# Filler products, split scores and values by DMA in the first chunk of a fused attention and feed-forward kernel

## The chip, the cores and the metric

The kernel runs on one core of a Trainium2 chip. The metric is device time in microseconds (us); lower is better. The core has five engines that work side by side, each through its own queue in order: TensorE (PE, matrix products, with its weight loads listed as PEld), VectorE (DVE), ScalarE (ACT), GpSimd (POOL) and SyncE (SP, which here issues every DMA). A float32 product is two instructions on PE in the profile, one in the type float32r is one.

## The reference

Windowed attention with block summaries, then a feed-forward layer with a squared ReLU. Batch 4, 8 heads, 768 positions, head size 64.

```python
k_sum = k.reshape(B, H, 24, 32, D).max(axis=3)      # block maxima of the keys
v_sum = v.reshape(B, H, 24, 32, D).mean(axis=3)     # block means of the values
scores_l = where(|i - j| < 16, q @ k.T / 8, -1e9)   # near keys
scores_s = q @ k_sum.T / 8 + log(32)                # block maxima
a = softmax(concatenate([scores_l, scores_s]))
x = (a @ concatenate([v, v_sum])) -> (3072, 512)
h = x @ w_in                                        # 512 -> 2048
out = (s * relu(h)**2 + b) @ w_out                  # 2048 -> 512
```

## The kernel before

The 3072 rows are cut into 12 chunks of 256 (`c`), three to a batch. A chunk's attention goes by head pairs `p` = 0..3: scores of four blocks of 64 queries against 96 near keys and 24 block maxima (`scores`), mask, scale and row minimum on DVE (`masked`), exponentials on ACT (`exps`), the division on DVE (`normalize`), transposes on PE (`transposes`), their copy on ACT (`turned`), products with 96 near values and 24 block means (`values`), and the copy of the result to the tile `x`, or to `xh` and `xl` (`attended`). The feed-forward layer walks 16 slices `f` of the hidden size: `hidden` (PE, tile `ph`), `activate` (ACT, then DVE in chunk 0, tiles `r` and `g`), `project` (PE, tile `po`), which runs two steps behind.

The weights arrive as 64-bit numbers in 32 tiles of 512 KB (`load_weights`, tile `wraw`). Each is scaled on ACT (`scale_weights`, two instructions, L116 and L117) and put together on DVE (`convert_weights`, L130, L132, L134, into `wf_in` or `wf_out`) while chunk 0 runs. Chunk 0 works in float32; later ones use two float32r halves.

The order of each engine's queue is written out by hand. `plan` maps a step to a list; within a step, entries are sorted by class (loads, splits, attention, weights, hidden, attention on PE, activation, projection, eviction), and nothing is reordered afterwards. Step -99 holds the string `FIRST_ORDER`, read from left to right: a letter is a stage, the digit its pair or weight slice.

- `q` loads keys and queries of a pair of chunk 0 (`kq`); `K` is `k_max` (L159), `S` both halves of `scores` (L269 near keys, L270 block maxima), `M` `masked` (L285), `E` `exps` (L298), `N` `normalize` (L305 to L308), `T` `transposes` (L314), `C` `turned` (L321).
- `r` loads rows of v (tile `vn`), `R0` to `R2` are products that average them (`mean_of_rows`, L202), `R3` copies the means to the tile `vsum` on ACT (L209).
- `v` loads near values into a tile `vw`, `F` is `fill_v` (L244: two copies that put each mean into `vw` four times, on DVE in chunks 0 and 1), `V` is `values` (L334), `X` `attended` (L347).
- `i`, `o` load weights; `A` scales one tile, `B` converts one, `D` two of a slice; `G0` is `fill_k` of chunk 1, pair 0 (L239); `u` loads queries and keys of a unit of chunk 1 (tile `qk`).

After that, step i runs `hidden`, `activate` for slice i of chunk 0, and chunk 1's attention is spread over steps 0 to 15 with offsets `lags`: its `scores(1,0)` stands on PE right behind `hidden(0,0)`, its four `fill_v` on DVE at steps 4, 7, 10 and 12, its loads of `vw` on SP at steps 0, 3, 6 and 8. The tile `vw` has four buffers, so the one of chunk 1, pair p comes free when `values(0,p)` is done. A tile pool with one buffer in PSUM (`ps_t`) holds the transposes.

Of the kernel before, what the change touches and what calls it, by code (L numbers as in the profile page):

```python
# [10 lines left out]
F32 = mybir.dt.float32  # L11
# [7 lines left out]
P = 128  # L19
B, H, S, D = 4, 8, 768, 64  # L20
# [3 lines left out]
SUB = 64  # L24
WIN = SUB + 2 * WINDOW
NB = S // BLOCK
KR = WIN + NB
NSUB = 4
# [11 lines left out]
def win_start(st):  # L40
    return min(max(SUB * st - WINDOW, 0), S - WIN)
# [3 lines left out]
def windowed_attention_then_relu2_ffn(ctx, tc, qk, vwin, kt, vt, kq, vrow, wp, sb, out):  # L45


    nc = tc.nc

    const = ctx.enter_context(tc.tile_pool(name="const", bufs=1))  # L50
# [8 lines left out]
    ps_t = ctx.enter_context(tc.tile_pool(name="ps_t", bufs=1, space=bass.MemoryType.PSUM))  # L59
# [6 lines left out]
    def make_mask(name, shifts):  # L66
        m = const.tile([P, KR], F32, name=name)
        nc.gpsimd.memset(m, 0.0)
        nc.gpsimd.memset(m[:, WIN:KR], 8.0 * math.log(BLOCK))
        for p0, shift in zip((0, 64), shifts):  # L70
            h = m[p0 : p0 + 64, 0:WIN]
            for sign in (1, -1):
                nc.gpsimd.affine_select(
                    out=h, in_=h, compare_op=ALU.is_gt, fill=NEG,
                    base=WINDOW + sign * shift, pattern=[[-sign, WIN]], channel_multiplier=sign,
                )
        return m

    mask_first = make_mask("mask_first", (0, WINDOW))
    mask_mid = make_mask("mask_mid", (WINDOW, WINDOW))  # L80
    make_identity(nc, ident)
# [7 lines left out]
    def at(step, order, fn, *args):  # L89
        plan[step].append((order, len(plan[step]), fn, args))  # L90
# [5 lines left out]
    for base, sign in ((0, 1), (BLOCK - 1, -1)):  # L96
        nc.gpsimd.affine_select(
            out=mean4[:, KR - 4 : KR], in_=mean4[:, KR - 4 : KR], compare_op=ALU.is_ge, fill=0.0,
            base=base, pattern=[[-sign * BLOCK, 4]], channel_multiplier=sign,
# [5 lines left out]
    def load_weights(key):  # L105
        side, f = key
        w_raw[key] = slots.tile([P, 512, 2], U32, name="wraw", tag="slot")
        src = wp[f, 0 if side == "in" else 1].bitcast(U32).rearrange("p (n w) -> p n w", w=2)
        nc.sync.dma_start(w_raw[key], src)
# [40 lines left out]
    kraw, ksum, vraw, vhalf, vsum = {}, {}, {}, {}, {}  # L150
# [42 lines left out]
    def load_scalars():  # L193
        nc.sync.dma_start(sb_col, sb.partition_broadcast(P))

    pm = []

    def mean_of_rows(n):
# [13 lines left out]
    def place(c):  # L212
        return c // PER_B, c % PER_B

    qk_t, vw_t, ps_of, pr_of, mn_of, sm_of, pt_of, pT_of, o_of, xt = ({} for _ in range(10))
# [7 lines left out]
    def load_unit(c, p):  # L223
        t = p3.tile([P, T + NSUB * KR], F32, name="qk", bufs=4)
        nc.sync.dma_start(t, qk[c - 1, p])
        qk_t[c, p] = t[:, 0:T], t[:, T:].rearrange("p (i k) -> p i k", k=KR)

    def load_values(c, p):
        v = p3.tile([KR, 2, NSUB, D], F32, name="vw", bufs=4)
        nc.sync.dma_start(v[0:WIN], vwin[c, p])  # L230
        vw_t[c, p] = v

    def filler(c):
        return nc.vector if c < 2 else nc.gpsimd
# [5 lines left out]

    def fill_v(c, p):
        bi, _ = place(c)
        for e in range(2):
            filler(c).tensor_copy(  # L244
                vw_t[c, p][WIN:KR, e],
                vsum[bi][WIN : WIN + NB, 2 * p + e, :].unsqueeze(1).to_broadcast([NB, NSUB, D]),
            )

    def scores(c, p, j):
        q, kw = qk_t[c, p]  # L250
        if j == 0:
            if c == 0 and p % 2:
                both = [ps_h.tile([P, T], F32, name="ps", tag="ph") for _ in range(2)]
                ps_of[c, p] = [t[:, : 2 * KR].rearrange("p (j k) -> p j k", k=KR) for t in both]
            elif c < 2:
                ps_of[c, p] = [ps_s.tile([P, 4, KR], F32, name="ps", tag="ps") for _ in range(2)]
            elif p % 2 == 0:
                both = [ps_s.tile([P, 4, KR], F32, name="ps", tag="ps") for _ in range(2)]
                ps_of[c, p], ps_of[c, p + 1] = [t[:, :2] for t in both], [t[:, 2:] for t in both]
        for e in range(2):  # L260
            r = slice(64 * e, 64 * e + 64)
            for a in range(2):
                i = 2 * j + a
                o, qi = ps_of[c, p][e][64 * a : 64 * a + 64, j], q[r, i * SUB : (i + 1) * SUB]
                if c > 0:
                    nc.tensor.matmul(o, qi, kw[r, i, :], start=True, stop=True)  # L266
                    continue
                w = win_start(i)
                nc.tensor.matmul(o[:, :WIN], qi, kraw[0, p][r, w : w + WIN], start=True, stop=True)  # L269
                nc.tensor.matmul(o[:, WIN:], qi, ksum[0, p][r], start=True, stop=True)  # L270

    def masked(c, p, j):
        _, ci = place(c)
# [129 lines left out]
    def evict(c):  # L403
# [8 lines left out]
    LOAD, SPLIT, ATT, WEIGHTS, HID, PE_ATT, CHAIN, PROJ, EVICT = range(9)  # L412


    FIRST, FIRST_SCALED, FIRST_TURNED = -100, 8, 2
    FIRST_ORDER = (
# [3 lines left out]
    )  # L420
    loads = {
        "q": load_first, "r": load_rows, "v": lambda p: load_values(0, p), "s": lambda _: load_scalars(),
        "i": lambda f: load_weights(("in", f)), "o": lambda f: load_weights(("out", f)),
        "u": lambda p: load_unit(1, p),
    }
    stages = {"K": k_max, "N": normalize, "F": fill_v, "T": transposes, "C": turned, "V": values, "X": attended}
    halves = {"S": scores, "M": masked, "E": exps}
    for n, name in enumerate(FIRST_ORDER.split()):
        kind, i = name[0], int(name[1:])
        if kind in loads:  # L430
            at(FIRST + 1, n, loads[kind], i)
        elif kind == "R":
            at(FIRST + 1, n, *((mean_of_rows, i) if i < 3 else (mean_done,)))
        elif kind == "A":
            at(FIRST + 1, n, scale_weights, ("in" if i % 2 == 0 else "out", i // 2))
        elif kind == "G":
            at(FIRST + 1, n, fill_k, 1, i)
        elif kind == "B":
            at(FIRST + 1, n, convert_weights, ("in" if i % 2 == 0 else "out", i // 2))
        elif kind == "D":  # L440
            at(FIRST + 1, n, convert_weights, ("in", i), ("out", i))
        elif kind in halves:
            for j in range(2):
                at(FIRST + 1, n, halves[kind], 0, i, j)
        else:
            at(FIRST + 1, n, stages[kind], 0, i)
    for c in range(1, NC):
        bi, ci = place(c)
        for p in range(NPAIR):
            if c == 1:  # L450

                base, v_at = (0, 3, 6, 8)[p], 0
                lags = (1, 2, 2, 3, 4, 4, 5, 6, 7)
            else:

                base, v_at = NF * (c - 1) - 2 + 8 * (p // 2), 3 * (p % 2)
                lags = ((1, 2, 2, 3, 6, 4, 5, 8, 9), (2, 3, 4, 5, 6, 6, 7, 8, 9))[p % 2]
            m, e0, e1, n, fv, tr, tu, va, xa = (base + lag for lag in lags)
            if ci == 0:
                at(base - 7, LOAD, load_k, bi, p)  # L460
                at(base - 2, ATT, k_max, bi, p)
                if p < 2:
                    for third in range(3):
                        at(base + v_at - 5 + third, LOAD, load_v, bi, p, third)
                        at(base + v_at - 1 + third // 2, ATT, v_sum, bi, p, third)
                    at(base + v_at + 1, ATT, v_mean, bi, p)
            if (c, p) not in ((1, 0),):
                at(base - 6, LOAD, load_unit, c, p)
            at(base + v_at, LOAD, load_values, c, p)
            if (c, p) != (1, 0):  # L470
                at(base - (1 if c > 1 else 2), ATT, fill_k, c, p)
            for j in range(2):
                at(base, PE_ATT, scores, c, p, j)
                at(m, ATT, masked, c, p, j)
                at((e0, e1)[j], ATT, exps, c, p, j)
            at(n, ATT, normalize, c, p)
            at(fv, ATT, fill_v, c, p)
            at(tr, PE_ATT, transposes, c, p)
            at(tu, ATT, turned, c, p)
            at(va, PE_ATT, values, c, p)  # L480
            if c < 2 or p % 2 == 0:
                at(xa, ATT, attended, c, p)
# [10 lines left out]
    for i in range(NC * NF):  # L493
        c, f = divmod(i, NF)
# [64 lines left out]
```

## Time and profile before

| what | value |
|---|---|
| median of 3 runs | 651.89 us (650.99 to 652.12) |
| the profiled execution | 652.11 us, span 650.4 us |
| busy share of the span | PE 97%, weight loads 85%, DVE 51%, ACT 51%, POOL 23% |
| DMA | 63.25 MB, mean 97 GB/s over the span |
| granted TensorE clock, mean | 0.997 |

The page divides the span into 40 slices of 16 us. PE shows 6 and 7 tenths in the first two and 9 or more in the others; DMA moves 324 to 389 GB/s in the first four slices and far less afterwards; DVE and ACT are full in slices three to five. So the first 90 us differ from the rest: there the weights arrive and are converted.

### The profile page before, as it was taken

What the parts mean: (1) busy time and instruction counts of PE and PEld (TensorE: products, weight loads), DVE (VectorE), ACT (ScalarE), POOL (GpSimd) and SP (SyncE); (2) the same over time, 40 slices, a digit from 0 to 9 for tenths busy, and PEclk for the clock granted to TensorE, in tenths of its full rate; (3) what the DMA queues carried; (4) which work ended last, traced back from release to release, by engine and by line L of the source; (5) the groups of instructions that cost most, each with busy time, mean ns of one, the idle gap of its engine ahead of it and who ended that gap; (6) DMA issues with size and microseconds to landing.
All of it is one profiled execution on the core that took longest, in us unless ns stands there. A gap on an engine that the chain in (4) does not pass through costs nothing.

```text
span 650.4 us, 13951 instructions
## 1 busy us (share of the span) xinstructions
PE 633.2 (97%) x5164; PEld 551.1 (85%) x5164; DVE 333.8 (51%) x1102; ACT 331.1 (51%) x972; POOL 152.5 (23%) x324
## 2 busy tenths in 40 slices
PE   6799999999999999999999999999999999999997
PEld 3565568899999999999999999999998989999996
DVE  5799997876433434356434344356443343342221
ACT  3899958745436435445445345254444444443322
POOL 3000004233133132231331331331322312312221
PEclk9999999999999999999999999999999999999999
DMA  8999405035203203224402300403510320100000
GB/s 324 389 386 349 122 2 185 2 102 184 78 1 104 72 3 126 59 76 142 146 1 65 112 1 33 154 10 119 179 56 2 105 71 2 57 3 1 32 2 33
DMA packets 25604, 63.25 MB, mean 97 GB/s; under 512 B 3968, under 2 KB 3968, under 8 KB 25536
## 3 DMA queue, kind: packets, MB, share of 16 engines
q1 hardware_dynamic: 25536, 62.36, 29.0%
q8 instruction: 41, 0.67, 0.4%
q14 instruction: 27, 0.22, 0.1%
HBM read 55.90 MB, written 6.29 MB: 96 GB/s over the span
## 4 chain that ended last, share of the span: by engine, by line
PE 88%; DVE 9%; DMA 1%; issue 1%; ACT 1%; SPq 0%; DVEq 0%
PE po L398 39%; PE ph L364 38%; PE pav L334 4%; PE ps L266 3%; PE pt L314 3%; DVE wf_in L132 1%; DVE wf_out L134 1%; DVE wf_out L132 1%; PE pm L202 1%; DMA vn<-in_vrow_dram 1%; DVE wf_in L134 1%; DVE wf_in L130 1%; DVE wf_out L130 1%; DVE g L375 1%; DVE vw L244 1%
## 5 line engine op out<-in xcount | busy, mean ns | idle before, releaser
L371 ACT ACTIVATE r<-ph 128x256 f32<-128x256 f32 x192 | 73.5, 383 | 286.4 <-PE ph L364 248.1
L381 DVE CAST gh<-g 128x256 fp32r<-128x256 f32 x176 | 52.7, 299 | 288.9 <-POOL g L379 262.1
L379 POOL TENSOR_SCALAR g<-r,sb_col 128x256 f32<-128x256 f32 x176 | 100.4, 570 | 423.8 <-ACT r L372 354.4
L398 PE MATMUL po<-wh,gl 128*128 128x512 f32 x352 | 142.9, 406 | 0.0
L398 PE MATMUL po<-wh,gh 128*128 128x512 f32 x352 | 138.7, 394 | 0.0
L398 PE MATMUL po<-wl_out,gh 128*128 128x512 f32 x352 | 138.1, 392 | 0.0
L364 PEld LDWEIGHTS ph<-xh,wl_in 128*128 128x128 f32 x704 | 107.6, 188 | 16.0 <-ACT r L372 0.7
L364 PE MATMUL ph<-xh,wl_in 128*128 128x256 f32 x704 | 113.1, 283 | 0.0
L364 PE MATMUL ph<-xl,wh 128*128 128x256 f32 x704 | 109.2, 277 | 0.0
L364 PE MATMUL ph<-xh,wh 128*128 128x256 f32 x704 | 108.8, 277 | 0.0
L364 PEld LDWEIGHTS ph<-xl,wh 128*128 128x128 f32 x704 | 95.1, 189 | 0.0
L364 PEld LDWEIGHTS ph<-xh,wh 128*128 128x128 f32 x704 | 92.9, 188 | 0.0
L372 ACT ACTIVATE r<-r 128x256 f32<-128x256 f32 x192 | 80.2, 418 | 6.1
L383 DVE TENSOR_TENSOR gl<-g,gh 128x256 fp32r<-128x256 f32 x176 | 76.4, 434 | 6.0
L398 PEld LDWEIGHTS po<-wh,gh 128*128 128x128 f32 x352 | 66.2, 188 | 13.8
L398 PEld LDWEIGHTS po<-wh,gl 128*128 128x128 f32 x352 | 66.1, 188 | 11.0 <-DVE gh L381 2.9
L398 PEld LDWEIGHTS po<-wl_out,gh 128*128 128x128 f32 x352 | 66.3, 188 | 7.8
L298 ACT ACTIVATE pr<-pr,mn 128x120 f32<-128x120 f32 x176 | 67.1, 383 | 3.4 <-DVE mn L285 3.4
L364 PEld LDWEIGHTS ph<-x,wf_in 128*128 128x128 f32 x128 | 24.8, 199 | 15.9 <-issue 6.3
L244 POOL COPY vw<-vsum 24x256 f32<-24x256 f32 x80 | 36.6, 497 | 1.3
L364 PE MATMUL ph<-x,wf_in 128*128 128x256 f32 x128 | 32.4, 400 | 4.5 <-DVE wf_in L134 3.7
L298 ACT ACTIVATION_READ_ACCUMULATOR pr<-pr,mn 128x1 f32 x176 | 33.1, 188 | 0.0
(70 smaller groups left out, 606.2 us busy)
## 6 DMA issues: line engine op xcount, KB each, us to landing
wraw<-in_wp_dram SPq DMA_DIRECT2D x32, 512.0 KB, 10.0
qk<-in_qk_dram SPq DMA_DIRECT2D x44, 368.0 KB, 5.1
vw<-in_vwin_dram SPq DMA_DIRECT2D x48, 192.0 KB, 4.9
out_dram<-o SPq DMA_DIRECT2D x24, 256.0 KB, 2.0
kraw<-in_kt_dram SPq DMA_DIRECT2D x12, 384.0 KB, 3.1
vraw<-in_vt_dram SPq DMA_DIRECT2D x12, 252.0 KB, 4.1
kq<-in_kq_dram SPq DMA_DIRECT2D x4, 512.0 KB, 4.3
vraw<-in_vt_dram SPq DMA_DIRECT2D x6, 264.0 KB, 6.8
```

Of the source, the lines that this page charges most:

```text
L244: filler(c).tensor_copy(vw_t[c, p][WIN:KR, e], vsum[bi][WIN : WIN + NB, 2 * p + e, :].unsqueeze(1).to_broadcast([NB, NSUB, D]),)
L266: nc.tensor.matmul(o, qi, kw[r, i, :], start=True, stop=True)
L298: nc.scalar.activation(pr, pr, AF.Exp, bias=mn_of[c, p][:, n : n + 1], scale=-1.0, accum_out=sm_of[c, p][:, n : n + 1])
L314: nc.tensor.transpose(pt_of[c, p][:KR, n * P : (n + 1) * P], pr[:, n, :], ident)
L334: nc.tensor.matmul(o[64 * e : 64 * e + 64, i * SUB : (i + 1) * SUB], vw[:, e, i, :], pT[:, e * T + i * SUB : e * T + (i + 1) * SUB], start ...
L364: nc.tensor.matmul(ph, w[:, kc * P : (kc + 1) * P], x[:, kc], start=(n == 0), stop=(n == len(terms) - 1))
L371: nc.scalar.activation(r, ph, AF.Relu)
L372: nc.scalar.activation(r, r, AF.Square)
L379: nc.gpsimd.tensor_scalar(g, r, s_col, b_col, ALU.mult, ALU.add)
L381: nc.vector.tensor_copy(gh, g)
L383: nc.vector.tensor_tensor(gl, g, gh.bitcast(F32), ALU.subtract)
L398: nc.tensor.matmul(po[t], a[:, t * P : (t + 1) * P], w, start=(f == 0 and n == 0), stop=(f == NF - 1 and n == len(terms) - 1),)
```

## The change

Five things change in chunk 0's start and in chunk 1:

1. DVE writes a tile of ones. New entries `W` (`keep_warm`) issue products of that tile with itself into the PSUM buffer of the transposes; nothing reads them. `W8` stands ahead of the first scores, `W1` behind those of pair 0, `W3` behind those of pair 1.
2. The products with the block maxima leave `scores` and become entries of their own, `Z`, so that near-key products no longer stand behind `k_max`.
3. The order of `FIRST_ORDER` changes: `R0` moves behind the scores of pair 2, `R1` behind the first transposes, `B0` ahead of the fills, `G0` behind `D1`, `u1` ahead of `i4`.
4. Chunk 1's four `load_values` move from steps 0 to 8 to entries `y0` to `y3` around `i5 o5`.
5. Chunk 1's `fill_v` becomes two DMAs on SP for each pair (24 rows, four times 256 bytes each), in place of two copies on DVE.

```diff
+    ones = const.tile([P, P], F32, name="ones")
+    nc.vector.memset(ones, 1.0)
...
+    def keep_warm(n):
+
+        t = ps_t.tile([P, 4 * P], F32, name="warm", tag="pt")
+        for _ in range(n):
+            nc.tensor.matmul(t[:, :P], ones, ones, start=True, stop=True)
+
...
     def fill_v(c, p):
         bi, _ = place(c)
+        if c == 1:
+            means = vsum[bi][WIN : WIN + NB, 2 * p : 2 * p + 2, :].unsqueeze(2).to_broadcast([NB, 2, NSUB, D])
+            for e in range(2):
+                nc.sync.dma_start(vw_t[c, p][WIN:KR, e], means[:, e])
+            return
...
+    def scores_of_maxima(p):
+        q, _ = qk_t[0, p]
+        for i in range(NSUB):
+            for e in range(2):
+                r = slice(64 * e, 64 * e + 64)
+                o = ps_of[0, p][e][64 * (i % 2) : 64 * (i % 2) + 64, i // 2]
+                nc.tensor.matmul(o[:, WIN:], q[r, i * SUB : (i + 1) * SUB], ksum[0, p][r], start=True, stop=True)
...
                 nc.tensor.matmul(o[:, :WIN], qi, kraw[0, p][r, w : w + WIN], start=True, stop=True)
-                nc.tensor.matmul(o[:, WIN:], qi, ksum[0, p][r], start=True, stop=True)
...
-        "K0 S0 K1 S1 M0 E0 K2 i2 M1 E1 o2 R0 S2 N0 T0 C0 K3 M2 E2 S3 i3 u0 N1 T1 R1 C1 M3 E3 R2 N2 T2 A0 C2 o3 i4 o4 "
-        "N3 T3 R3 C3 F0 V0 F1 X0 V1 F2 B0 A1 X1 V2 F3 X2 V3 B1 X3 A2 A3 G0 D1 i5 o5 A4 A5 A6 A7"
+        "W8 K0 S0 W1 Z0 K1 S1 Z1 M0 E0 W3 K2 i2 M1 E1 o2 S2 Z2 R0 N0 M2 E2 K3 S3 Z3 u0 i3 T0 R1 C0 N1 M3 E3 R2 A0 N2 T1 C1 o3 u1 i4 o4 "
+        "B0 T2 R3 C2 N3 F0 V0 F1 T3 X0 V1 F2 C3 X1 V2 F3 A1 X2 V3 B1 X3 A2 A3 D1 G0 y0 y1 i5 o5 y2 y3 A4 A5 A6 A7"
...
+        "u": lambda p: load_unit(1, p), "y": lambda p: (load_values(1, p), fill_v(1, p)),
...
-            if (c, p) not in ((1, 0),):
+            if (c, p) not in ((1, 0), (1, 1)):
                 at(base - 6, LOAD, load_unit, c, p)
-            at(base + v_at, LOAD, load_values, c, p)
+            if c != 1:
+                at(base + v_at, LOAD, load_values, c, p)
...
-            at(fv, ATT, fill_v, c, p)
+            if c != 1:
+                at(fv, ATT, fill_v, c, p)
```

More of the change, by code (lines that the diff above doesn't have):

```diff
@@ L423, in windowed_attention_then_relu2_ffn @@
         "i": lambda f: load_weights(("in", f)), "o": lambda f: load_weights(("out", f)),
-        "u": lambda p: load_unit(1, p),
+        "u": lambda p: load_unit(1, p), "y": lambda p: (load_values(1, p), fill_v(1, p)),
     }
@@ L435, in windowed_attention_then_relu2_ffn @@
             at(FIRST + 1, n, scale_weights, ("in" if i % 2 == 0 else "out", i // 2))
+        elif kind == "W":
+            at(FIRST + 1, n, keep_warm, i)
+        elif kind == "Z":
+            at(FIRST + 1, n, scores_of_maxima, i)
         elif kind == "G":
```

## The prediction, made before the changed kernel ran

> **What bounds the kernel now.** I read the page first, then a table of stretches of time, then PE's waits, then the engines' rows for the first 50 us. From the page:
>
> ```profile
> PE 633.2 (97%) x5164; PEld 551.1 (85%) x5164; DVE 333.8 (51%) x1102; ACT 331.1 (51%) x972; POOL 152.5 (23%) x324
> ```
>
> PE bounds the whole: what it waits, and what it does slowly, is the only time to win. The table shows where (length, then PE, PEld, DVE, ACT, POOL busy, granted clock, DMA share, GB/s):
>
> ```profile
> 8.00:25.95 17.95, 14.18 (x157) 8.49 (x157) 11.95 (x51) 11.44 (x40) 0.00 (x0) 1.00 1.03 373
> 25.95:50.00 24.05, 21.46 (x102) 14.20 (x100) 23.38 (x65) 23.79 (x58) 0.00 (x0) 0.93 1.03 391
> 50.00:76.00 26.00, 24.91 (x144) 15.88 (x144) 25.77 (x71) 23.67 (x60) 1.15 (x2) 1.00 0.88 275
> ```
>
> Up to 25.95 no engine is full: it is a chain of handovers. From 25.95 to 50 DVE, ACT and DMA are full together (23.38 and 23.79 of 24.05, share 1.03), and PE waits a little for each. So an earlier start counts only as far as all of them follow. PE's waits (total, times, longest):
>
> ```profile
> PE ph L364 <- DVE wf_in L134: 3.7, 4, 1.9
> PE pav L334 <- DVE vw L244: 1.5, 2, 1.2
> ...
> PE ph L364 <- ACT r L371: 0.7, 1, 0.7
> ```
>
> All of them fall before 88 us, so what PE has won by then stays won to the end. PE's own rows:
>
> ```profile
> 25.95 1.99 PE L364 MATMUL ph<-x,wf_in 128*128 128x256 f32 x8
> 27.87 0.64 PE L266 MATMUL ps<-qk 64*64 64x120 f32 x16
> 30.45 5.41 PE L364 MATMUL ph<-x,wf_in 128*128 128x256 f32 x16 [1.94 <-DVE wf_in L134]
> ...
> 50.73 0.45 PE L364 MATMUL ph<-x,wf_in 128*128 128x256 f32 x1 [1.00 <-DVE wf_in L134]
> ```
>
> `hidden(0,0)` starts at 25.95; the next waits 1.94 for its weights, and 16 instructions then take 5.41 where 8 took 1.99. The clock of that stretch, from the table:
>
> ```profile
> 31.00:32.00 1.00, 1.00 (x4) 0.82 (x3) 1.00 (x3) 1.00 (x3) 0.00 (x0) 0.50 1.05 405
> ```
>
> **The start, step by step.** PE is slow once more before that:
>
> ```profile
> 8.82 3.74 PE L202 MATMUL pm<-vn,mean 128*120 128x512 f32 x4 [0.92 <-DMA vn<-in_vrow_dram]
> ...
> 16.24 3.60 PE L202 MATMUL pm<-vn,mean 128*120 128x512 f32 x8
> 19.68 0.60 PE L314 MATMUL pt<-ident,pr 128*120 128x128 f32 x4
> ```
>
> `R0` takes 0.93 an instruction, `R1` and `R2` 0.45. So the clock is at half speed at 8.82 and full at 16.24 (the table's clock column reads 1.00 at 8.82, so it does not show this). Unbroken work opens it, and a pause of 2 us can shut it.
>
> `W8` is eight float32 products, 16 instructions. Four transposes of 128x128 take 0.45 to 0.60 at full speed, 0.11 each where they follow each other, so 0.23 at half speed and 3.7 in all. Bounds: 1.8 (full speed) and 7.4 (weight load not overlapped); I take 3.7, since the transposes have a load and a product of that size. With the ones written near 0.8, W8 runs from 1.1 to 4.7. The keys of pair 0 land at 4.3 and PE waits for them anyway: W8 costs 0.4 on the path, 3 us at the upper bound. `S0 W1 Z0 S1 Z1 W3` keep PE without a pause to 8; the clock opens between 4.5 and 8. From there the chain goes by rows such as these, of DVE and of ACT:
>
> ```profile
> 10.21 0.95 DVE L159 TENSOR_REDUCE ksum<-kq 128x24 f32<-128x768 f32 x1
> 13.75 0.28 DVE L285 CUSTOM_DVE_ANT_0 pr<-ps,mask_first 128x120 f32<-128x120 f32 x1 [2.59 <-PE ps L270]
> ```
>
> ```profile
> 16.93 0.40 ACT L298 ACTIVATE pr<-pr 128x120 f32<-128x120 f32 x1
> ...
> 18.45 0.66 ACT L116 ACTIVATE wraw<-wraw 128x512 f32<-128x512 f32 x1
> 19.01 0.67 ACT L117 ACTIVATE wraw<-wraw 128x512 int32<-128x512 uint32 x1
> 20.31 0.59 ACT L321 COPY pT<-pt 120x512 f32<-120x512 f32 x1 [0.63 <-PE pt L314]
> 20.92 0.58 ACT L209 COPY vsum<-pm 24x512 f32<-24x512 f32 x1
> ```
>
> `K` 0.95, `M` 0.9 (four of about 0.2), `N` 1.0, `E` 1.6, `A` 1.13, `C` and `R3` 0.59, `R1` with `R2` 3.43, `T` 0.45, `V` 0.65, `X` 0.3, `B` 1.9:
> - DVE: K1 to 6.5, M0 7.5, K2 8.4, M1 9.2, N0 10.2, M2 11.0, K3 12.0; Z3 on PE to 12.35. R0 lies beside this (8.7 to 10.6) and no longer holds pair 2's scores to 12.56.
> - PE: T0 12.8, R1 and R2 to 16.25, T1 16.7. ACT: E3 15.0, A0 16.15, C1 17.3, R3 17.9, C2 18.5.
> - DVE: B0 15.65 to 17.5, N3 18.45, fills (0.5 a pair) to 20.45. PE: V0 18.95 to 19.6, T3, V1, V2, V3 to 22.0. ACT: A1 to 22.1, X2 and X3 22.7.
>
> So `hidden(0,0)` starts at 21.9 for 25.95, **4.05 earlier**, and ACT is free of X3 at 22.7 for 26.4, 3.7 earlier. DVE before:
>
> ```profile
> 27.22 0.20 DVE L239 COPY qk<-ksum 128x96 f32<-128x96 f32 x1
> 27.34 0.42 DVE L130 TENSOR_SCALAR wf_in<-wraw 128x512 uint32<-128x512 uint32 x1
> 28.16 0.43 DVE L130 TENSOR_SCALAR wf_out<-wraw 128x512 uint32<-128x512 uint32 x1 [0.41 <-ACT wraw L116]
> ```
>
> D1's second tile waits for ACT's A3 at 28.16 and DVE is full from there on. A3 is now half done at 24.45: DVE is also **3.7 earlier**.
>
> **What speaks against it: G0.** The row at 27.22 is `G0`, which `scores(1,0)` needs. It now stands behind D1, which ends at 24.45 + 2.75 = 27.2. PE is done with `hidden(0,0)` at 23.7 and waits 3.7, to 27.4, where it waited 1.94, and all of PE's queue stands behind those scores. The weights of `hidden(0,1)` are there at 26.75; it starts at 28.3. The clock shuts in such a pause. With half speed to about 32 (eight at 0.45, eight at 0.235) the second and third hidden products end at 33.8 for 35.86: PE keeps **2.05**. Bounds: 2.55 if the clock opens at 30.8, 0.95 if at 34.2.
>
> The Trainium skill, "TensorE: Matmul & The Clock Gate", Part 1 (The HAM clock gate), says that the clock halves after an idle window of about 3.4 us, and that the windows run freely. Here it shut after a pause of 1.94, so the trace is stricter than the page. By the page a pause of 3.7 rarely covers a whole window, the clock would mostly stay open, and the sum would be that of the open-clock rival below.
>
> **Fills and loads by DMA.** The copies, as a group and in the chain that ended last:
>
> ```profile
> L244 DVE COPY vw<-vsum x16: 282/283/291, 21.5 to 82.3; 24x256 f32<-24x256 f32 x16
> ```
>
> ```profile
> 46.20 0.33 DVE g L375
> 46.53 0.03 issue
> 46.56 0.50 DVE vw L244 x2
> ```
>
> Eight of the 16 are chunk 1's. Two cost 0.50 and handovers of 0.03 on a full DVE, so each pair leaves 0.55: 2.2 in all, at steps 4, 7, 10, 12.
>
> The price is on DMA. SP has eight transfers out at a time, so an issue tells when the eighth before it landed:
>
> ```profile
> 26.31 6.31 SPq L109 DMA_DIRECT2D wraw<-in_wp_dram  x6
> 33.53 0.33 SPq L230 DMA_DIRECT2D vw<-in_vwin_dram  x1
> 34.48 0.33 SPq L225 DMA_DIRECT2D qk<-in_qk_dram  x1
> 35.82 0.33 SPq L109 DMA_DIRECT2D wraw<-in_wp_dram  x1
> ```
>
> ```profile
> 41.37 0.68 ACT L116 ACTIVATE wraw<-wraw 128x512 f32<-128x512 f32 x1
> ```
>
> `i6` was issued at 26.31, landed near 35.82 and was scaled at 41.37: 5.5 in hand. Now ACT comes 3.7 earlier, and four `vw` (0.79 MB at about 0.405 MB/us: 1.95) and eight fills stand ahead of it. A fill is 96 pieces of 256 bytes. The nearest rows are the copies of 24 such pieces, by their issue and by the DMA share while they run alone:
>
> ```profile
> L183 SPq DMA_DIRECT2D vsum<-vmean x24: 713/718/1221, 148.5 to 459.9; - x24
> ```
>
> ```profile
> 151.50:152.00 0.50, 0.50 (x5) 0.46 (x4) 0.50 (x1) 0.23 (x1) 0.47 (x1) 1.00 0.06 12
> ```
>
> 12 GB/s for 0.5 us is one copy of 6 KB, in 6% of 16 engines: 20 ns a piece. 768 pieces are 1.0 over 16 engines. Upper bound: SP's 0.72 for each fill as if nothing ran beside it, 5.8. I take 1.0, since seven other transfers are out while SP issues. Then `i6` lands at 38.8, 1.1 after ACT would take it at 37.7. `u1` ahead of `i4` (0.37 MB, 0.9) uses up the reserve of `o3` to `o4` and costs ACT some 0.4. SP itself: `y0` stands behind V0 (19.6) and `y3` behind V3 (22.0), both before SP has room for them (from about 24), so those waits are hidden; if V3 came after 32, SP would starve the weights queued behind it.
>
> ACT's lead thus falls to 2.4 around `i6`. Its `r` feeds `g` on DVE, and `g` of slices 0 to 2 comes hard behind its `r`: I take 0.4 off DVE's lead for it, an allowance. DVE is then 3.3 ahead, and with the fills gone 3.85, 4.4 and more.
>
> **Sum for PE.** 2.05 in front. Of the waits of 3.7 on DVE, 1.94 is spent again at G0; 1.74 go, and the 0.69 on ACT: 2.05 + 1.74 + 0.69 = 4.48, capped by DVE's 4.4. Less 0.2 for handovers: 4.2. The profiled execution was 652.11 (span 650.4), 0.22 above the median of 651.89: 652.11 - 4.2 = 647.9, by the median 647.7; I say **647.8**.
>
> **Rivals.** *The products do not open the clock early.* For it: the table does not show this gate at the start, and products that fill little of PE may not count. Against: the work from 8.82 on opened it before. R0 would take 3.74 from 10.0, Z3 ends 1.9 later, and PE keeps 0.15 + 1.74 + 0.69: 649.5.
>
> *Fills half hidden.* At 0.3 to 0.6 each, `i6` lands 1.4 to 3.8 later still and DVE waits on `g`: 649 to 651.5.
>
> *The fills starve ACT (slower).* `g` of slice 3 ran at 46.20; behind `i6` stand two tiles (2.4) and `r` (0.8), so `g` is later than before if `i6` lands after 43.0, that is, if a fill holds the stream for over 0.65. For it: SP's 0.72. Against: 6% busy. At 0.72 to 0.9 it lands at 43.5 to 45, and the kernel takes 652.4 to 653.5. The Trainium skill, "DMA: Bandwidth & Descriptors", Specifications, asks for 512 bytes a piece for line rate, which speaks for this rival; the row's 20 ns do not.
>
> *The clock stays open and DMA is no later.* PE then follows DVE's 5.0 to 5.7: 646.4 to 647.1.
>
> *The lead is lost on the way,* to a wait that I do not see: within 0.2% of before.
>
> **Numbers.** Mine 0.58 (646.9 to 648.9, by the clock's bounds and DVE's cap); clock late 0.08; half hidden 0.14; slower 0.07; open clock 0.10; lost 0.03. The range that leaves out under 2 in 10 is 646.4 to 650.3. A difference under 0.2% (1.3 us) cannot be told from none. Faster: 0.58 + 0.08 + 0.10 + 0.12 of the half hidden = 0.88; same 0.05; slower 0.07.
>
> **What would show it.** R0 at 0.45 an instruction, near 9; `hidden(0,0)` near 22; `scores(1,0)` waiting some 3.7 for L239, and half clock behind it; no L244 on DVE after 21; `i6` landing near 39; no PE wait on L134 after 35. I am wrong if V3 or the tiles of slices 4 to 7 come later than said, or if W8 lasts beyond 6.

## The result and the profile after

| | before | after |
|---|---|---|
| median | 652.00 us (6 runs, 650.99 to 652.40) | 655.56 us (6 runs, 654.10 to 657.61) |
| ratio, 95% interval | | 1.0056 (1.0043 to 1.0069) |
| profiled execution (span) | 652.11 us (650.4) | 657.61 us (655.9) |

The kernel is 3.6 us slower; the forecast was 4.2 faster, with 650.3 as the upper end. The profiled execution of after was the longest of its six, 2.05 above the median, so its pauses are a little longer than the median's. Three executions on record (one of before, one each of `e_undo45` and `e_pool_vw128`, 704 to 1611 us) ran far slower than all others and count in no ratio.

The page, engine by engine. PE's busy time is 5.3 us more than before, and its 24 further instructions are the fillers, of which `W8` takes 3.78:

```profile
PE 638.5 (97%) x5188; PEld 557.0 (85%) x5188; DVE 331.8 (51%) x1095; ACT 332.4 (51%) x972; POOL 153.2 (23%) x324
```

PE's waits from 20 to 100 us (total, times, longest). Before had 3.7 on the converted weights in four pieces; now there is one of 6.1:

```profile
PE ph L384 <- DVE wf_in L136: 6.1, 1, 6.1
PE ps L287 <- DVE qk L247: 3.2, 1, 3.2
PE ph L384 <- ACT r L391: 0.9, 1, 0.9
```

(In the changed kernel L384 is `hidden`, L247 `fill_k`, L118 and L119 `scale_weights`, L132 to L136 `convert_weights`, L391 to L395 `activate`, L111 `load_weights`, L238 `load_values`, L233 `load_unit`, L254 the fills' DMAs.) PE's rows in order of time, in brackets the pause ahead of the row and who ended it:

```profile
1.12 3.78 PE L202 MATMUL warm<-ones 128*128 128x128 f32 x16 [1.12 <-DVE ones L80]
9.39 1.98 PE L210 MATMUL pm<-vn,mean 128*120 128x512 f32 x4
13.35 3.60 PE L210 MATMUL pm<-vn,mean 128*120 128x512 f32 x8
18.06 0.65 PE L334 MATMUL pt<-ident,pr 128*120 128x128 f32 x4 [0.68 <-ACT pT L341]
19.59 0.88 PE L354 MATMUL pav<-pT,vw 120*64 120x64 f32 x16 [0.88 <-DVE vw L257]
21.32 2.81 PE L354 MATMUL pav<-pT,vw 120*64 120x64 f32 x48
24.07 1.99 PE L384 MATMUL ph<-x,wf_in 128*128 128x256 f32 x8
29.29 0.64 PE L287 MATMUL ps<-qk 64*64 64x120 f32 x16 [3.23 <-DVE qk L247]
29.86 5.41 PE L384 MATMUL ph<-x,wf_in 128*128 128x256 f32 x16
46.41 1.99 PE L384 MATMUL ph<-x,wf_in 128*128 128x256 f32 x8 [0.93 <-ACT r L391]
56.23 3.75 PE L384 MATMUL ph<-x,wf_in 128*128 128x256 f32 x8 [6.10 <-DVE wf_in L136]
```

The fillers do open the clock: `R0` takes 1.98 where it took 3.74. `hidden(0,0)` starts at 24.07 (before 25.95), but of that lead only 0.59 is left at `hidden(0,1)` (29.86 for 30.45). Then slice 6 starts at 56.23, where before had it at 50.73: 5.5 behind. It also takes 3.75 where an earlier eight took 1.99, because the clock shut in the pause (granted clock 0.50 from 55 to 60). That is 7.3 us behind. Before's later pauses of 0.36, 0.69 and 0.45 are gone, 1.5 of the 1.8 by which this exceeds the growth of the span, 5.5.

Who holds PE for 6.10 is in the chain that ended last, here from 42.96 on:

```profile
42.96 10.41 DMA qk<-in_qk_dram
53.37 0.02 issue
53.39 0.21 DVE qk L247
53.60 0.34 DVE wf_in L132
```

It is not a weight tile. It is `qk`, the queries and keys of chunk 1's third pair (`u2`, 0.37 MB), 10.41 us from issue to landing. On DVE, which works in order, the copy `fill_k` (53.39) stands ahead of the conversion of slice 6. It waits 5.33 for `qk`, and slice 6's weights wait behind it:

```profile
DVE qk L247 <- DMA qk<-in_qk_dram: 5.3, 1, 5.3
DVE g L395 <- ACT r L392: 2.6, 4, 1.1
```

Why `u2` lands so late stands in SP's queue (start, time on SP):

```profile
24.44 0.33 SPq L111 DMA_DIRECT2D wraw<-in_wp_dram  x1
25.70 0.33 SPq L238 DMA_DIRECT2D vw<-in_vwin_dram  x1
26.96 1.83 SPq L254 DMA_DIRECT2D vw<-vsum  x2
...
38.29 1.63 SPq L254 DMA_DIRECT2D vw<-vsum  x2
39.97 2.93 SPq L111 DMA_DIRECT2D wraw<-in_wp_dram  x6
42.96 0.43 SPq L233 DMA_DIRECT2D qk<-in_qk_dram  x1
```

From 25.70 to 39.97 SP works through `y0` to `y3` with `i5 o5` between. `i6` (39.97) had been issued at 26.31 before. `u2` had been issued at 34.48, a row that the prediction shows and does not use; now it goes out at 42.96, behind six tiles of 512 KB. The table by stretches (length, PE, PEld, DVE, ACT, POOL busy, granted clock, DMA share, GB/s) shows that the stream of loads itself became slower in that time; before it moved 406 and 407 GB/s in the first two of these stretches:

```profile
30.00:35.00 5.00, 5.00 (x16) 4.11 (x17) 4.92 (x18) 3.59 (x7) 0.00 (x0) 0.66 0.80 217
35.00:40.00 5.00, 5.00 (x32) 3.05 (x31) 4.74 (x11) 4.89 (x15) 0.00 (x0) 1.00 0.90 278
40.00:45.00 5.00, 4.96 (x19) 2.69 (x17) 3.84 (x10) 2.99 (x7) 0.00 (x0) 1.00 0.79 261
```

### The profile page after: what moved, and what is told of

Its sections match the earlier page's. It is cut to its first block, busy times and chain, and to the rows that moved or that the text cites. A ratio compares the mean times of both kernels' runs of the same rounds, so it can differ in the third digit from the quotient of the medians.

```text
span 655.9 us, 14003 instructions
## 1 busy us (share of the span) xinstructions
PE 638.5 (97%) x5188; PEld 557.0 (85%) x5188; DVE 331.8 (51%) x1095; ACT 332.4 (51%) x972; POOL 153.2 (23%) x324
## 4 chain that ended last, share of the span: by engine, by line
PE 92%; DMA 3%; DVE 2%; ACT 1%; POOL 1%; issue 0%; SPq 0%; POOLq 0%; DVEq 0%
PE po L418 41%; PE ph L384 40%; PE pav L354 4%; PE ps L287 3%; PE pt L334 3%; DMA wraw<-in_wp_dram 2%; DMA qk<-in_qk_dram 2%; ACT pr L318 0%; DVE pr L305 0%; ACT wraw L118 0%; DVE ksum L161 0%; ACT wraw L119 0%; DVE pr L328 0%; DVE wf_in L136 0%; DVE wf_in L134 0%
## 5 line engine op out<-in xcount | busy, mean ns | idle before, releaser
L391 ACT ACTIVATE r<-ph 128x256 f32<-128x256 f32 x192 | 73.5, 383 | 290.2 <-PE ph L384 253.9
L384 PEld LDWEIGHTS ph<-xh,wl_in 128*128 128x128 f32 x704 | 107.6, 188 | 16.0 <-ACT r L392 0.7
L384 PE MATMUL ph<-xh,wl_in 128*128 128x256 f32 x704 | 113.1, 283 | 0.0
L384 PE MATMUL ph<-xl,wh 128*128 128x256 f32 x704 | 109.2, 277 | 0.0
L384 PE MATMUL ph<-xh,wh 128*128 128x256 f32 x704 | 108.8, 277 | 0.0
L384 PEld LDWEIGHTS ph<-xl,wh 128*128 128x128 f32 x704 | 95.1, 189 | 0.0
L384 PEld LDWEIGHTS ph<-xh,wh 128*128 128x128 f32 x704 | 92.9, 188 | 0.0
L384 PEld LDWEIGHTS ph<-x,wf_in 128*128 128x128 f32 x128 | 26.2, 208 | 18.0 <-ACT r L392 7.6
L384 PE MATMUL ph<-x,wf_in 128*128 128x256 f32 x128 | 34.0, 415 | 7.1 <-DVE wf_in L136 6.1
```

Source lines behind the costliest of these rows:

```text
L384: nc.tensor.matmul(ph, w[:, kc * P : (kc + 1) * P], x[:, kc], start=(n == 0), stop=(n == len(terms) - 1))
L391: nc.scalar.activation(r, ph, AF.Relu)
```

## The experiments

Theory A: parts 4 and 5 put a megabyte and eight fills ahead of the stream, and `u2` behind them is what DVE and PE wait for. Rivals: the shut clock and the late `G0` at the start cost the time (B); the fills as transfers are dear in themselves (C); the loads of `vw` are dear in themselves (D). Each ratio is against the kernel before on the same chip, with its 95% interval. The letters in the expectations were given run by run and are not these. Line numbers shift by a few between these kernels: `hidden` lies between L364 and L387, `fill_k` is L239, L247 or L250.

### One load earlier, parts 4 and 5 undone, parts 4 and 5 alone

`e_u2early`, the changed kernel with `u2` ahead of `y0`:

```diff
-... A2 A3 D1 G0 y0 y1 i5 o5 y2 y3 A4 A5 A6 A7"
+... A2 A3 D1 G0 u2 y0 y1 i5 o5 y2 y3 A4 A5 A6 A7"
```

> The changed kernel, with the load of chunk 1's third unit (u2) moved ahead of y0; nothing else. Theory A (the y entries hold SP back, since only eight transfers are out at a time, and u2, queued behind them, keeps DVE waiting 5.33 us at fill_k of pair 2 and PE 6.10 us behind that): that wait goes, DVE's next wait is for weight slice 6, scaled near 47, and the kernel takes 650.0 to 652.5. Theory B (the 256-byte pieces cost DMA bandwidth, so all weights are late): slice 6 and 7 come as late as u2 did, and the kernel stays at 654.5 to 656.

Measured: 652.26, ratio 1.0008 (0.9998 to 1.0017). Moving one load of 0.37 MB takes back 3.3 of the 3.6 us. The wait for `qk` is down to 0.3. The stream is as late as it was, and now ACT feels it at the weight tiles (ACT's waits of this kernel; the changed kernel has 3.8 in three here):

```profile
ACT wraw L118 <- DMA wraw<-in_wp_dram: 5.2, 4, 2.5
```

So the place of `u2` sets which consumer stalls; that the stream is late is a second matter.

`e_undo45`, the changed kernel with `y0` to `y3` out of the order and chunk 1's loads and fills where before has them:

```diff
-... A2 A3 D1 G0 y0 y1 i5 o5 y2 y3 A4 A5 A6 A7"
+... A2 A3 D1 G0 i5 o5 A4 A5 A6 A7"
```

> The changed kernel with parts 4 and 5 undone: chunk 1's values are loaded at steps 0, 3, 6, 8 and its fills are DVE copies again; filler products, split scores and the new order stay (G0 behind D1, u1 ahead of i4). Theory A: the whole loss is gone; PE keeps the 0.6 us by which its second hidden product is earlier and DVE its 1.9 us, so 649.5 to 651.5. Theory C (the loss comes from the order: G0 behind D1 and the clock that shuts twice): it stays slower than before, 653 to 656.

Measured: 650.64, ratio 0.9978 (0.9969 to 0.9988). Parts 1 to 3 alone gain 1.3 us against the 651.89 of that comparison (0.8 to 2.0 by the interval), so the start is not what makes the change slower: rival B falls.

`e_only45`, the kernel before with parts 4 and 5 alone:

```diff
-... X3 A2 A3 G0 D1 i5 o5 A4 A5 A6 A7"
+... X3 A2 A3 G0 D1 y0 y1 i5 o5 y2 y3 A4 A5 A6 A7"
```

> The kernel before with parts 4 and 5 alone: y0 y1 ahead of i5 o5 and y2 y3 behind them in the old order, fills by DMA; no filler products, scores whole, old order else. Theory A: u2 lands near 53 here too, DVE arrives at fill_k of pair 2 near 47.5 and waits about 5.5 us: 655 to 657.5. Theory C (the new order is what loses): 650 to 652.5, since DVE is 2.2 us lighter.

Measured: 655.77, ratio 1.0062 (1.0047 to 1.0077). The time came as expected, the place did not. In this order `u1` also stands behind the `y`, and it is `u1` that is waited for:

```profile
40.09 0.21 DVE L239 COPY qk<-ksum 128x96 f32<-128x96 f32 x1 [5.08 <-DMA qk<-in_qk_dram]
```

### Loads and fills apart

`e_tiny8`: `y0` to `y3` load `vw`; the two fills of each become two transfers of one row of 64 bytes into tiles that nothing reads, and chunk 1's fills go back to DVE at their old steps.

```diff
-        "y": lambda p: (load_values(1, p), fill_v(1, p)),
+        "y": lambda p: (load_values(1, p), tiny(p)),
```

> The changed kernel, with each fill's DMA replaced by one of a single row of 64 bytes to a tile that nothing reads, at the same place of SP's order; the fills are DVE copies again at their old steps (so the output is the reference's). Eight places in SP's order as before, but 8 pieces in place of 768. Theory A (places, not pieces): the gap at SP remains, u2 is issued near 42 and DVE waits about 5 us: 655 to 658. Theory B (pieces): like the kernel without parts 4 and 5, 649.5 to 652.

Measured: 654.25, ratio 1.0042 (1.0026 to 1.0059), between the two forecasts.

`e_loads_early`: the same without the eight small transfers.

```diff
-        "y": lambda p: (load_values(1, p), fill_v(1, p)),
+        "y": lambda p: load_values(1, p),
```

> The changed kernel with the fills as DVE copies at their old steps; the four loads of chunk 1's values stay at y0 to y3. Theory A (the eight fills, as places in SP's order, are the loss): only 0.8 MB stand ahead of u2, it is some 2 us later and still in time: 650.2 to 651.5, as without parts 4 and 5. Rival D (the early loads themselves put u2 too late): like the run with eight tiny transfers, 653.5 to 655.

Measured: 654.40, ratio 1.0040 (1.0028 to 1.0053). That eight more places in the queue were the cost is thereby out: with them and without them the time is the same, although the stream does show them (230 and 259 GB/s from 30 to 40 us with them, 281 and 278 without). The four early loads alone cost 654.40 - 650.64 = 3.8 us. Their stretches (of `e_loads_early`) speak for rival D:

```profile
30.00:35.00 5.00, 5.00 (x18) 3.94 (x18) 5.00 (x18) 3.18 (x7) 0.00 (x0) 0.80 1.04 281
35.00:40.00 5.00, 5.00 (x31) 2.72 (x29) 4.38 (x9) 4.15 (x14) 0.00 (x0) 1.00 1.05 278
```

The DMA share is 1.04 and 1.05, full, and yet only 281 and 278 GB/s move. A `vw` load is 96 rows of 2 KB, one to a partition.

`e_vw128`: `e_loads_early`, with `vw` loaded as 128 rows in every chunk, 32 of them zeros that nothing reads. A load then moves 256 KB in place of 192.

```diff
-        v = p3.tile([KR, 2, NSUB, D], F32, name="vw", bufs=4)
-        nc.sync.dma_start(v[0:WIN], vwin[c, p])
+        v = p3.tile([P, 2, NSUB, D], F32, name="vw", bufs=4)
+        nc.sync.dma_start(v, vwin[c, p])
```

> The run with early loads and fills on DVE, with each load of near values made 128 rows high (zeros below row 96; 256 KB in place of 192 KB); all chunks alike. In the traces a 96-row load lowers the stream for 3 us, from about 405 to 266, 308 and 328 GB/s, and so takes 1.36 us where its bytes would take 0.49. If the 96 rows cause that, a load now takes 0.65, u2 lands some 2.8 us earlier and the kernel takes 651.0 to 652.7. If it is the 2 KB pieces (or anything else of these loads), it stays at 653.8 to 655.5.

Measured: 650.39, ratio 0.9974 (0.9963 to 0.9984). A third more bytes, and 4.0 us less than `e_loads_early`, more than forecast. The same stretches:

```profile
30.00:35.00 5.00, 5.00 (x17) 3.77 (x17) 5.00 (x19) 4.71 (x13) 0.00 (x0) 0.77 1.04 403
35.00:40.00 5.00, 5.00 (x32) 2.92 (x31) 4.93 (x12) 4.87 (x14) 0.00 (x0) 1.00 1.03 407
```

Same share, 403 and 407 GB/s. So it was the 96 rows that made the loads dear; that chunk 0's loads have 128 rows here too does not explain it, since `e_pool_vw128` below has them as well and gains nothing. The slow loads also slow what runs beside them: in the traces' records of single pieces, from 30 to 35 us, a 2 KB piece of `vw` takes 133 ns (median) with 96 rows and 86 with 128, and a 4 KB piece of a weight tile beside it 228 and 164. Why 96 rows are slow no run here shows. The Trainium skill, "DMA: Bandwidth & Descriptors", section "Why a DMA increments its semaphore by 16 and not by 1", says that a tile of 96 partitions is spread over all 16 engines; the full share agrees, so engines left idle are not the reason.

`e_fills_early`: the eight fill DMAs at `y0` to `y3`, the loads at their old steps.

```diff
-        "y": lambda p: (load_values(1, p), fill_v(1, p)),
+        "y": lambda p: (new_values(1, p), fill_v(1, p)),
```

> The changed kernel with the four loads back at steps 0, 3, 6, 8 and only the eight fill DMAs at y0 to y3. If the fills hold the stream up by themselves (u2 was some 3 us later in the changed kernel than with eight tiny transfers): u2 lands near 47.5 to 48, DVE waits 1 to 2 us for it: 650.5 to 652.5. If they cost next to nothing, as I predicted, and the loads alone are the loss: DVE is 2.2 us lighter, 648.8 to 650.3.

Measured: 651.65, ratio 0.9996 (0.9986 to 1.0007), 1.0 above `e_undo45`. That is the net of DVE's relief and of what the fills do to the stream:

```profile
35.00:40.00 5.00, 5.00 (x33) 3.31 (x32) 5.00 (x11) 4.97 (x16) 0.00 (x0) 1.00 0.57 173
```

Share 0.57: the stream runs dry while SP issues fills. SP needs 0.8 us for each in the changed kernel (min, median, max in ns), against 0.33 for a tile of 512 KB:

```profile
L254 SPq DMA_DIRECT2D vw<-vsum x8: 778/800/980, 27.0 to 39.1; - x8
```

`e_fills_gpq`: `e_fills_early` with these DMAs issued from GpSimd's queue.

```diff
-                nc.sync.dma_start(vw_t[c, p][WIN:KR, e], means[:, e])
+                nc.gpsimd.dma_start(vw_t[c, p][WIN:KR, e], means[:, e])
```

> As the run with only the fills early (loads at their old steps), but the eight fill DMAs are issued from GpSimd's queue in place of SP's. Same 768 pieces on the same DMA engines, no place and no time in SP's order. If SP's order is what hurts: u2 lands in time, DVE is 2.2 us lighter: 648.0 to 649.8. If the pieces hurt: as with SP, 651 to 652.5.

Measured: 649.67, ratio 0.9962 (0.9947 to 0.9976). The move off SP's queue is thus worth about 2.0 us. Not all of it need be SP's order: the profile counts 256 packets for these fills on GpSimd's queue, where the same fills add 864 packets on SP's, so their form on the wire differs too. The transfers still weigh on the stream, 312 GB/s at full share where before moved 406:

```profile
25.00:30.00 5.00, 1.59 (x21) 0.98 (x21) 4.53 (x11) 5.00 (x10) 1.42 (x3) 1.00 1.02 312
```

`e_fills_steps`: the changed kernel with loads and fill DMAs both at the old steps of chunk 1's attention (`y0` to `y3` out of the order).

```diff
-            if c != 1:
+            if True:
                 at(base + v_at, LOAD, load_values, c, p)
...
-            if c != 1:
+            if True:
                 at(fv, ATT, fill_v, c, p)
```

> The changed kernel with chunk 1's loads back at steps 0, 3, 6, 8 and its fills still by DMA, but at their old steps 4, 7, 10, 12 in SP's order, two at a time among 512 KB tiles. Theory A (it is the cluster ahead of slices 5 to 8 and u2 that hurts): DVE is 2.2 us lighter at little cost: 648.5 to 650.5. Theory B (fills cost wherever they stand): 651.5 to 654.

Measured: 660.66, ratio 1.0143 (1.0125 to 1.0161); neither forecast. The first of the fills is issued at 52.42, needs the backlog of the stream ahead of it, and PE, which has it in `values(1,0)`, stands still for 11.77 (PE's row; the trace names a transfer of the same queue):

```profile
62.80 1.37 PE L354 MATMUL pav<-pT,vw 120*64 120x64 f32 x16 [11.77 <-DMA wraw<-in_wp_dram]
```

So a fill by DMA must be issued some 10 us ahead here, and where it is (`e_fills_early`), it holds up what follows: neither of the two places tried on SP is good for part 5.

`e_after_mended`: the whole change, with 128-row loads and the fills on GpSimd's queue.

```diff
-        v = p3.tile([KR, 2, NSUB, D], F32, name="vw", bufs=4)
+        v = p3.tile([P, 2, NSUB, D], F32, name="vw", bufs=4)
...
-                nc.sync.dma_start(vw_t[c, p][WIN:KR, e], means[:, e])
+                nc.gpsimd.dma_start(vw_t[c, p][WIN:KR, e], means[:, e])
```

> The changed kernel with its early loads 128 rows high and its fills issued from GpSimd's queue; all else of the change stays (filler products, order, G0 behind D1, loads at y0 to y3). If the slow loads and the fills in SP's order are the whole loss: u2 some 2.5 us later than before, in time or 1 us late, DVE 2.2 us lighter: 648.2 to 650.0. If something else of the change loses time: above 651.

Measured: 651.37, ratio 0.9989 (0.9979 to 1.0000). It is 4.2 us better than the change, but it lies where the second forecast has it: the slow loads and SP's order are not the whole loss. `u2` still comes 3.3 late on DVE, and PE waits 2.6 behind it (the wait is put down to ACT's scaling, but the conversion of slice 6 behind `fill_k` ends last, at 50.76). The moved megabyte is still ahead of `u2`, and the stream moves 400, 383 and 331 GB/s in the three stretches from 30 to 45.

### The start

`e_nowarm`: `e_undo45` without `W8`, `W1`, `W3`.

```diff
-        "W8 K0 S0 W1 Z0 K1 S1 Z1 M0 E0 W3 K2 ...
+        "K0 S0 Z0 K1 S1 Z1 M0 E0 K2 ...
```

> Parts 4 and 5 undone and the filler products left out (no W8, W1, W3); split scores and the new order stay. If the fillers matter by the clock (my prediction: R0 at half speed costs 1.9 us on the path): 651.7 to 653. If the gain of the start is lost again before 30 us by G0 and DVE: 650.2 to 651.2, as with them.

Measured: 650.38, ratio 0.9982 (0.9972 to 0.9991), 0.26 below `e_undo45`, less than the 1.3 us that can be told. No gain from the fillers shows at the end. `R0` is slow again (8.89, 3.77 us), yet `hidden(0,0)` starts at 23.61; with fillers in `e_undo45` at 23.93. In that trace what the fillers gain at `R0` is given back at 20 to 24, as in the changed kernel, whose clock there is

```profile
21.00:22.00 1.00, 1.00 (x14) 0.68 (x14) 0.00 (x0) 0.57 (x1) 0.00 (x0) 0.50 1.00 397
```

while in `e_nowarm` the table reads 1.00 from 20 to 25. The fillers are not the reason for that: with the same fillers and the same order up to `G0`, the clock also reads 1.00 from 18 to 26 in the traces of `e_loads_early`, `e_vw128` and `e_after_mended`, and `hidden(0,0)` starts at 22.58, 22.30 and 22.23 there. So with an open clock the start is 1.0 to 1.4 earlier than in `e_nowarm`, and so is `scores(1,0)` (28.20 to 28.53 for 29.57). What that would be worth at the end no run shows by itself.

`e_g0first`: `e_undo45` with `G0` ahead of `D1`, as before had it.

```diff
-... A2 A3 D1 G0 i5 o5 A4 A5 A6 A7"
+... A2 A3 G0 D1 i5 o5 A4 A5 A6 A7"
```

> Parts 4 and 5 undone and G0 ahead of D1 as in the kernel before. If G0 behind D1 costs PE what it waits (3.8 us at the scores of chunk 1, of which some 1.2 stand ahead of its weights): 648.8 to 649.8. If DVE sets the pace behind it anyway: 650.0 to 651.0, no different from the same kernel with G0 behind D1 (650.6).

Measured: 651.05, ratio 0.9992 (0.9983 to 1.0001): no gain against the 650.64 of `e_undo45`. The wait on `G0` is gone, and PE waits for converted weights in its place:

```profile
PE ph L379 <- DVE wf_in L136: 5.2, 5, 2.1
```

DVE sets the pace of this stretch, and the order of two of its items moves PE's pause, not its end.

### Relieving DVE in another way

If DVE sets the pace, the gain of part 5 should be there when the fills leave DVE without touching the stream. GpSimd does nothing from 8 to 50 us (POOL 0.00 in the prediction's table). `e_pool`: `e_nowarm` with chunk 1's fills as copies on GpSimd (`filler` gives those of later chunks to GpSimd already).

```diff
-            filler(c).tensor_copy(
+            (nc.gpsimd if c > 0 else nc.vector).tensor_copy(
```

> Parts 4 and 5 undone, no filler products, chunk 1's fills as copies on GpSimd, which is idle there: DVE loses the 2.2 us without any transfer. If DVE sets the pace up to 80 us: 648.3 to 649.6. If ACT or the weights do: 649.8 to 650.8, as with the copies on DVE (650.4).

Measured: 647.99, ratio 0.9940 (0.9926 to 0.9953), the fastest here, 2.4 below `e_nowarm`. On PE only the wait on `G0` and two short ones are left between 20 and 100 us:

```profile
PE ps L282 <- DVE qk L247: 3.8, 1, 3.8
PE pav L349 <- DVE vw L252: 0.9, 1, 0.9
PE pav L349 <- DVE xl L364: 0.4, 1, 0.4
```

`e_pool_vw128`: `e_pool` with loads of 128 rows, as in `e_vw128`.

```diff
-        nc.sync.dma_start(v[0:WIN], vwin[c, p])
+        nc.sync.dma_start(v, vwin[c, p])
```

> The same with the loads of near values 128 rows high. If the loads' slow stretch matters in that order too: 0.3 to 1.0 us below the run before it; if DMA has room there: the same within 0.3 us.

Measured: 648.78, ratio 0.9949 (0.9936 to 0.9963), 0.8 above `e_pool`, which is neither forecast: nothing gained. Where the loads stand at the old steps, the stream's lateness is not what is waited for.

`e_before_pool`: the kernel before with chunk 1's copies on GpSimd, and nothing else.

```diff
-            filler(c).tensor_copy(
+            (nc.gpsimd if c > 0 else nc.vector).tensor_copy(
```

> The kernel before, unchanged but for chunk 1's fills as copies on GpSimd. If the gain of the run without parts 4 and 5 but with GpSimd copies (648.0) is the sum of the order's 1.5 and DVE's 2.4: 649.2 to 650.2. If only the two together give it (DVE is not the limit in the old order): 651.0 to 652.0.

Measured: 649.44, ratio 0.9962 (0.9948 to 0.9976): 2.7 of the 4.0 us by which `e_pool` beats before come from DVE's relief without any other change; the new order adds about 1.3.

## Why the prediction was wrong, point by point

**W8, the clock, R0: right.** 1.12 to 4.90 for 1.1 to 4.7, 3.78 for 3.7; `R0` at 0.50 an instruction, near 9; `R1` and `R2` 3.60 for 3.43.

**`hidden(0,0)` at 21.9: wrong by 2.2.** The chain was followed as if the clock, once open, stayed open. `V0` starts at 19.59 for 18.95, a lag of 0.64; the rest is lost after it, where the clock is at 0.50 and `V1` to `V3` take 2.81. It shut behind pauses of 0.68 and 0.88. In the trace of before it shut behind 1.94, and the prediction had asked what pauses of 2 us do, not what shorter ones do. Part of the 2.2 is the luck of the one execution that was profiled: `e_after_mended` has the same two pauses (0.68 and 0.88), its clock stays at 1.00, and its `hidden(0,0)` starts at 22.23, 0.3 behind the forecast (22.58 in `e_loads_early`, whose loads have 96 rows and whose clock stays open too). The Trainium skill, "TensorE: Matmul & The Clock Gate", Part 1, halves the clock after an idle window of about 3.4 us; the halving behind these two pauses does not agree with that, as the one behind 1.94 did not. What decides it stays open; the half-speed stretches last 3.4 us or a multiple of it (20.58 to 23.98 in the changed kernel, 27.76 to 34.58 in `e_nowarm`), so where a pause falls may count as well as its length.

**D1's second tile at 24.45, DVE 3.7 earlier: wrong by 1.8.** It runs at 26.28, waiting 0.49 for ACT. `scores(1,0)` waited 3.23 for `G0` as described (3.7 forecast), at half clock behind it, but to 29.29 instead of 27.4. Of the 2.05 kept by PE in front, 0.59 was there. The worry about `G0` behind `D1` was right as a row and beside the point as a cost: `e_g0first` gains nothing.

**Four loads at 1.95 us: mis-sized.** Bytes by the stream's rate gave 1.95; the loads cost 3.8 us of the kernel's time by themselves. The trace of before had the rows. Its load of `vw` issued at 33.53 was due in these stretches (beside `u2`, so the sum is an estimate):

```profile
40.00:41.00 1.00, 1.00 (x18) 0.60 (x15) 1.00 (x3) 1.00 (x3) 0.00 (x0) 1.00 1.08 266
41.00:42.00 1.00, 1.00 (x4) 0.52 (x3) 1.00 (x3) 0.97 (x4) 0.00 (x0) 1.00 1.05 308
42.00:43.00 1.00, 1.00 (x5) 0.68 (x5) 0.93 (x4) 1.00 (x3) 0.00 (x0) 1.00 1.02 328
43.00:44.00 1.00, 1.00 (x7) 0.82 (x6) 1.00 (x4) 0.99 (x3) 0.00 (x0) 1.00 1.01 374
```

Against 405 GB/s that is 139 + 97 + 77 + 31 = 344 KB less, 0.85 us, beside the load's own 0.49: 1.34 a load, 5.4 for four. An average of 391 GB/s over 24 us, as the prediction showed, hides such a dip.

**Fills at 1.0 us: mis-sized.** They were priced at 20 ns a piece from a stretch in which nothing else ran. That price held, 18 to 21 ns (medians in the changed kernel, 30 to 45 us); but SP's 0.72 (now 0.80) was set aside because seven other transfers would be out. They bring `e_fills_early` to 1.0 above `e_undo45` although DVE's relief is worth 2.4 by `e_pool`: about 3.4. Of this some 2.0 goes with SP's queue (`e_fills_gpq`), which leaves about 1.4; the split is rough, since `e_pool` also lacks the fillers and the fills on GpSimd's queue move in other packets. "Fills half hidden" and "the fills starve ACT" looked in the right place, but at `i6` alone.

**`i6` at 38.8, ACT starved there: wrong place, and the step that was missing.** `i6` lands at about 43.6, where ACT waits 1.98 for it; ACT also waits 1.33 for the tile of slice 4 and 0.53 for that of slice 7, the sign of being wrong that the prediction had named. The late tiles cost something by themselves: with `u2` ahead of them the kernel is still 1.6 above `e_undo45`, although DVE has no fills there. But the largest wait is another. The queue was followed to `i6` and to `g`, not past it to `u2`, which no term of the sum and no rival holds. Its price in this kernel is the 5.33 on DVE, the 6.10 on PE and the 1.76 of half clock behind them; `e_u2early` has 3.3 of it back.

**DVE's relief of 2.2: right in size** (2.4 in `e_pool`, 2.7 in `e_before_pool`), but the way that the change takes to it costs more than it brings.

The account. Read by the prediction's own terms, parts 1 to 3 were worth 3.5 (DVE's 3.7 less 0.2) and parts 4 and 5 another 0.7. Measured, parts 1 to 3 are worth 1.3, which is 2.2 short; parts 4 and 5 cost 655.56 - 650.64 = 4.9 (loads 3.8, fills net 1.0), which is 5.6 from a gain of 0.7. Together 7.8, the whole miss of 655.56 - 647.8. The intervals are some 0.6 us wide to each side, so the parts of this account are rough, and that loads and fills add up so well is partly chance: both act on the one queue.

Open: why 96 rows move at 0.7 of the rate; how the 3.4 of the fills divides more finely; what shuts the clock in one trace and not in another with the same pauses; why eight small transfers at the same places cost nothing on top of the early loads while eight fills do, beyond SP's 0.8 for each fill.

## What to carry to other kernels

When a transfer is moved ahead in a full, in-order stream, follow every later transfer to its first consumer, the small loads above all, and ask what stands behind that consumer on its engine; here a load of 0.37 MB, whose row the prediction shows but does not follow, stopped DVE and, behind it, PE. Price a moved load by what the stream does while such a load runs, in stretches of 1 us, not by its bytes. If an engine that sets the pace is to be relieved, look first for an idle engine that can do the same instruction: all five parts together lost 3.6 us, and chunk 1's copies moved to GpSimd gained 2.7 in the kernel before.

## What the runs showed of the hardware that was not expected

- A stretch with loads of 96 rows of 2 KB among 512 KB tiles holds all DMA engines busy (share 1.04) at 281 GB/s; with 128 rows the same stretch moves 403 GB/s. The weight tiles' pieces beside them take 228 ns in place of 164.
- A fill of 96 pieces of 256 bytes within the chip's memory holds SP for 0.80 us, a 512 KB load for 0.33 (0.55 for 64 bytes, in `e_tiny8`). Issued late in a full stream, its consumer waited 11.77.
- The clock can shut behind two pauses of 0.68 and 0.88 that are 1.5 us apart (changed kernel), and can stay open behind the same two (`e_after_mended`, `e_nowarm`); it shut behind 3.23 and 6.10 too.
